# A decode attention kernel that streams its cache through a five-slot ring: slots handed out by the program, w_down in one load, two small loads swapped, one more V tile halved

## The chip, the core and the metric

The kernel runs on one core of one Trainium2 chip. The metric is the device time of one execution in microseconds; the time of a kernel is the median of its runs. The core has a matrix engine (TensorE, PE in the profile), a vector engine (VectorE, DVE), a scalar engine (ScalarE, ACT), GpSimd (POOL), a queue processor that issues transfers (SyncE, SP) and 16 DMA engines, which carry every load from the chip's main memory (HBM) into the on-chip memory (SBUF).

## What is computed

One token is decoded. Part A is attention with 32 heads of width 128 over a cache of 65,536 positions, part B is a small gated feed-forward layer, and a sigmoid gate mixes the two:

```python
q = (x @ wq).reshape(32 heads, 128)             # x: 1 x 512, wq: 512 x 4096
scores = einsum("hd,hkd->hk", q, k_cache) * 128 ** -0.5
p = softmax(scores)
a = einsum("hk,hkd->hd", p, v_cache).reshape(1, 4096) @ wo       # wo: 4096 x 512
b = (silu(x @ w_gate) * (x @ w_up)) @ w_down    # 512 x 1792 twice, 1792 x 512
g = sigmoid((x * gate_w).sum())
out = g * a + (1 - g) * b
```

All inputs are bf16. The K cache and the V cache are 537 MB each, and every byte of them is used once; everything else together is some 14 MB.

## The kernel before, in words

**Tiles.** A tile is 16,384 positions of one head: 128 partitions, 128 positions of 128 numbers on each, 32 KB per partition, 4 MB in all. There are four tiles per head (`G`) and 128 K tiles and 128 V tiles (`N`). Each is fetched by one instruction on SP's queue (`load`, L102 to L109, the transfer itself on L108); a tuple `cuts` can divide a tile into several transfers. K0 comes in two halves, V126 in two halves, V127 in five pieces (32, 32, 32, 16 and 16 of its 128 columns); all others come whole.

**The ring.** The big loads share a pool of five slots of 32 KB per partition (`ring`, L58, `big`, L69). In the order of the program they are: wq (the query weights), K0, K1, w_gate with w_up (`gu_t`), w_down (`wd_t`), then K2, K3, and from there K and V tiles in turn, and last the second half of wo (`load_wo_end`). A new tile can be loaded into a slot once everything that used the slot's last tenant is done. The pool chooses the slot: it takes the one whose last use stands earliest in the program. SP works its queue strictly in order, so a load that waits for its slot holds back all loads behind it. Each transfer also reports to one of eight semaphores, taken in turn; a transfer waits until the one eight places before it has landed.

**The steps.** A list `steps` (L344 to L352) fixes what happens together: step n loads K tile n and, from n = 4 on, a V tile v which lags four tiles behind. From n = 40 on (`SPREAD`) a V tile is left out of some steps, until the lag is eight (`LAG`); the last eight steps have V tiles alone. In a step, DVE multiplies the K tile by the query in place (L240) and adds halves together down to a width of 16 (L244, `products`); PE adds the remaining 16 columns with an identity matrix into the scores (L254, `scores`). After the four tiles of a head come a maximum, an exponential on ACT (L279) and the sum (L288). PE multiplies V tiles by the probabilities (L302, `values`, 32 matmuls per tile). On PE the order within a step is: the finished head's column (`head_column`, L323), `values(v)`, then `scores(n)`, then the projection of a finished head with wo (L335, `project`). wo's first 16 heads come in four loads of 512 KB (`load_wo`, L167), the first of them in step 3; the last 16 heads come in five pieces behind V127 (L161).

**The feed-forward layer.** `feed_forward_in` (step 1) does the two first products, `feed_forward_mid` (step 2) silu, the product and the multiplication with w_down, `feed_forward_out` (step 3) the gate and the first addition into the final accumulator. For the multiplication with w_down the hidden vector is first rearranged from 128 partitions x 14 to 64 x 28 (L200 to L206), because w_down lies on 64 partitions, 28 rows of 1 KB each. It is loaded in eight transfers of eight partitions (L142 to L146); two of them are issued before K2, six behind K2.

**The small loads.** xT (x, 1 KB) is issued by ACT's queue at the very start (L76); it feeds `X_bc` (four copies on DVE, L91), which the query matmuls (L117) need. gwT (gate_w, 1 KB) is issued on SP's queue behind w_up (L149); it is first used in step 2 (L197).

**The end.** After V127's last matmul: `head_copy` of head 31 in two halves on ACT and DVE, four projections, head 31's column, twelve projections with wo's last half, a cast (L413) and the store of the output (L414).

Of the kernel before, what the change touches and what calls it, by code (L numbers as in the profile page):

```python
# [8 lines left out]
ACT = mybir.ActivationFunctionType  # L9
ALU = mybir.AluOpType  # L10
AXIS = mybir.AxisListType
P = 128
# [3 lines left out]
NB = 128  # L16
SLOTS = 5
# [8 lines left out]
def kernel(  # L26
# [14 lines left out]
    nc = tc.nc  # L41
    bf16 = mybir.dt.bfloat16
    f32 = mybir.dt.float32

    _, H, Sk, Dh = A_k_cache.shape
    D = A_x.shape[2]
    F = B_w_gate.shape[1]
    KT = D // P
    FT = F // P
    G = Sk // (NB * P)  # L50
    NBH = Sk // P
    N = H * G
# [2 lines left out]
    scale = float(Dh) ** -0.5  # L55

    consts = ctx.enter_context(tc.tile_pool(name="consts", bufs=1))
    ring = ctx.enter_context(tc.tile_pool(name="ring", bufs=SLOTS))  # L58
    small = ctx.enter_context(tc.tile_pool(name="small", bufs=2))
    ppool = ctx.enter_context(tc.tile_pool(name="ppool", bufs=3))  # L60
    wo_pool = ctx.enter_context(tc.tile_pool(name="wo_pool", bufs=2))
# [3 lines left out]
    psum_m = ctx.enter_context(tc.tile_pool(name="psum_m", bufs=2, space=bass.MemoryType.PSUM))  # L65

    ctx.enter_context(tc.manual_schedule())

    def big(name):  # L69
        return ring.tile([P, NB * Dh], bf16, name=name, tag="big")  # L70


    xT = consts.tile([P, KT], bf16, name="xT")
    gwT = consts.tile([P, KT], bf16, name="gwT")
    with nc.allow_non_contiguous_dma(reason="small"):
        nc.scalar.dma_start(out=xT, in_=A_x[0, 0, :].rearrange("(p t) -> p t", t=KT))  # L76
    wq_t = big("wq_t")
    wq_sb = wq_t[:, : KT * H * Dh].rearrange("p (t f) -> p t f", t=KT)
    nc.sync.dma_start(out=wq_sb, in_=A_wq.rearrange("(p t) f -> p t f", t=KT))

    ident_f = consts.tile([P, P], f32, name="ident_f")
    make_identity(nc, ident_f[:])
    ident_b = consts.tile([P, P], bf16, name="ident_b")
# [15 lines left out]

    K_tiles, V_tiles, S_tiles, P_tiles, O_tiles = {}, {}, {}, {}, {}  # L100

    def load(dst, cache, n, name, cuts=(0, NB)):  # L102
        h, g = divmod(n, G)
        t = big(name)
        view = t.rearrange("p (j d) -> p j d", d=Dh)
        src = cache[0, h, g * NB * P : (g + 1) * NB * P, :].rearrange("(p j) d -> p j d", j=NB)
        for a, b in zip(cuts[:-1], cuts[1:]):
            nc.sync.dma_start(out=view[:, a:b, :], in_=src[:, a:b, :])  # L108
        dst[n] = view  # L109

    load(K_tiles, A_k_cache, 0, "K_t", (0, NB // 2, NB))
    load(K_tiles, A_k_cache, 1, "K_t")

    def queries(g):
        qg_ps = psum_m.tile([P, QG * Dh], f32, name="qg_ps", tag="misc")
# [13 lines left out]
        queries(g)  # L129


    gu_t = big("gu_t")
    wgu_sb = gu_t[:, : 2 * KT * F].rearrange("p (w t f) -> p w t f", w=2, t=KT)
    nc.sync.dma_start(out=wgu_sb[:, 0], in_=B_w_gate.rearrange("(p t) f -> p t f", t=KT))
    nc.sync.dma_start(out=wgu_sb[:, 1], in_=B_w_up.rearrange("(p t) f -> p t f", t=KT))
    wd_t = big("wd_t")
    HP = P // 2
    GT = F // HP
    wd_sb = wd_t[:HP, : GT * D].rearrange("p (t n) -> p t n", t=GT)
    wd_rows = B_w_down.rearrange("(p t) n -> p t n", t=GT)  # L140

    def load_wd(*which):  # L142
        for i in which:
            lo = (0, 1, 2, 3, 32, 33, 34, 35)[i]
            part = slice(lo, lo + 29, 4)
            nc.sync.dma_start(out=wd_sb[part], in_=wd_rows[part])  # L146

    with nc.allow_non_contiguous_dma(reason="small"):
        nc.sync.dma_start(out=gwT, in_=gate_w.rearrange("(p t) -> p t", t=KT))  # L149
    load_wd(0, 1)  # L150
    WG = 4
    wo_tiles = {}

    WH = H // 2
    wo_end = []

    def load_wo_end(cuts):
        t = big("wo_t")[:, : (H - WH) * D].rearrange("p (h n) -> p h n", n=D)
        rows = A_wo[WH * P :, :].rearrange("(h p) n -> p h n", p=P)
        for a, b in zip(cuts[:-1], cuts[1:]):  # L160
            nc.sync.dma_start(out=t[:, a:b, :], in_=rows[:, a:b, :])  # L161
        wo_end.append(t)

    def load_wo(g):
        wo_tiles[g] = wo_pool.tile([P, WG, D], bf16, name="wo_sb")
        rows = A_wo[g * WG * P : (g + 1) * WG * P, :]
        nc.sync.dma_start(out=wo_tiles[g], in_=rows.rearrange("(h p) n -> p h n", p=P))  # L167
# [21 lines left out]
    def feed_forward_mid(gu_sb, eg):  # L189
        nc.vector.tensor_scalar_add(eg, eg, 1.0)  # L190
        nc.vector.reciprocal(eg, eg)
        hprod = consts.tile([P, FT], f32, name="hprod")
        nc.vector.tensor_tensor(out=hprod, in0=gu_sb[:, :FT], in1=eg, op=ALU.mult)
        hT = consts.tile([P, FT], bf16, name="hT")
        nc.vector.tensor_tensor(out=hT, in0=hprod, in1=gu_sb[:, FT:], op=ALU.mult)
        xg = consts.tile([P, KT], f32, name="xg")
        nc.vector.tensor_tensor(out=xg, in0=xT, in1=gwT, op=ALU.mult)  # L197
        xs = consts.tile([P, 1], f32, name="xs")
        nc.vector.tensor_reduce(out=xs, in_=xg, axis=AXIS.X, op=ALU.add)
        h_ps = psum_m.tile([HP, GT], f32, name="h_ps", tag="misc")  # L200
        for r in range(2):
            nc.tensor.matmul(
                h_ps[:, r * FT : (r + 1) * FT], lhsT=ident_b[:, r::2], rhs=hT, start=True, stop=True
            )
        h2 = consts.tile([HP, GT], bf16, name="h2")
        nc.scalar.activation(out=h2, in_=h_ps, func=ACT.Copy)  # L206
        b_ps = psum_m.tile([1, D], f32, name="b_ps", tag="misc")
        for t in range(GT):
            nc.tensor.matmul(  # L209
                b_ps, lhsT=h2[:, t : t + 1], rhs=wd_sb[:, t, :], start=(t == 0), stop=(t == GT - 1)  # L210
            )
        g_ps = psum_m.tile([P, 1], f32, name="g_ps", tag="misc")
        nc.tensor.matmul(g_ps, lhsT=ones_f, rhs=xs, start=True, stop=True)
        eg2 = consts.tile([P, 1], f32, name="eg2")
        nc.scalar.activation(out=eg2, in_=g_ps, func=ACT.Exp, scale=-1.0)
        return b_ps, eg2
# [13 lines left out]
    def products(n, a=0, b=NB):  # L230

        h = n // G
        K = K_tiles[n][:, a:b, :]
        qb = q_bc[:, h * Dh : (h + 1) * Dh]
        q_rep = bass.AP(
            tensor=qb.tensor,
            offset=qb.offset,
            ap=[list(qb.ap[0]), [0, b - a], [1, Dh]],
        )
        yield nc.vector.tensor_tensor(out=K, in0=K, in1=q_rep, op=ALU.mult)  # L240
        half = Dh
        while half > WIDTH:
            half //= 2
            yield nc.vector.tensor_tensor(  # L244
                out=K[:, :, 0:half], in0=K[:, :, 0:half], in1=K[:, :, half : 2 * half],
                op=ALU.add,
            )
# [97 lines left out]
    v = 0  # L345
# [8 lines left out]
    ff = done = tot_ps = None  # L354
    for n, v in steps:
        if n is not None and n > 1:
            load(K_tiles, A_k_cache, n, "K_t")
        if n == 2:
            load_wd(2, 3, 4, 5, 6, 7)
        if n == 3:  # L360
            load_wo(0)
        if v is not None:
            if v % (WG * G) == 2 * G and v // (WG * G) + 1 < WH // WG:
                load_wo(v // (WG * G) + 1)
            load(V_tiles, A_v_cache, v, "V_t", (0, NB) if v < N - 2 else (0, 64, NB) if v < N - 1 else (0, 32, 64, 96, 112, NB))
            if v == N - 1:
                load_wo_end((0, 4, 8, 12, 14, 16))
        if n == 2:
            ff = feed_forward_mid(*ff)
        halves = (0, NB // 2)  # L370
        vector = iter(()) if n is None else products(n)
        if n == 0:
            vector = (i for a in halves for i in products(n, a, a + NB // 2))
        top_of = None
        if n is None:
            top_of = H - 1 if S_tiles else None
        elif n % G == 0 and n > 0:
            top_of = n // G - 1
            vector = (i for a in halves for i in products(n, a, a + NB // 2))
        if top_of is not None:  # L380
            next(vector, None)
            mT_ps = row_max(top_of)
            next(vector, None)
            exponentials(top_of, mT_ps)
        for _ in vector:
            pass
        if n == 1:
            ff = feed_forward_in()
        if n == 3:
            feed_forward_out(*ff)  # L390
        if tot_ps is not None:
            weight(*tot_ps)
            tot_ps = None
        if done is not None:
            head_column(done, head_copy(done))
        if v is not None:
            values(v)
        if top_of is not None:
            tot_ps = top_of, total(top_of)
        if n is not None:  # L400
            scores(n)
        if done is not None and done < WH:
            project(done)
        done = v // G if v is not None and v % G == G - 1 else None
# [40 lines left out]
```

## Time and profile before

| | us |
|---|---|
| median of three runs (2533.16 to 2534.53) | 2533.54 |
| the profiled execution, its own time | 2534.51 |
| its span (first to last instruction) | 2532.6 |
| DVE busy in the span | 2175.5 |
| PE busy in the span | 1742.4 |
| ACT busy in the span | 75.9 |

The 16 DMA engines moved 1088.63 MB in the span, 430 GB/s in the mean. SP's queue carried 42,674 packets, which fill 99.7% of the 16 engines' time; 53 packets of 16 KB are instructions which the engines' own programs fetch. The mean granted clock of TensorE was 0.749 of full speed.

The profile gives busy times by engine and line, a picture of the span in 40 slices, the waits (who waited for whom), the chain of work that ended last, and a timeline. Times are microseconds from the start of the span. The trace also holds two lists which the views add up: one row for every packet of every DMA engine (start, duration, bytes), and the completion marks of the transfers. Each DMA engine that takes part in a transfer posts its own mark when its share has landed, so a transfer that runs on 16 engines has 16 marks, and the transfer counts as landed with the last of them. Neither list names the engine.

### The profile page before, as it was taken

How to read it: one execution, taken by the hardware profiler on the slowest of the kernel's cores; microseconds unless marked ns; L12 is line 12 of the kernel's file. 1: busy time of each engine (PE TensorE's matmuls, PEld its weight loads, DVE VectorE, ACT ScalarE, POOL GpSimd, SP SyncE). 2: the span in 40 equal slices, each digit the busy share in tenths (PEclk: the TensorE clock that was granted, in tenths of full speed). 3: DMA queues.
4: the chain of work that ended last, by engine and by line, in shares of the span. 5: the costliest groups of instructions: out<-in, count | busy, mean ns of one | idle time of the engine just before them, and what ended most of it. 6: DMA issues, size and time to landing. Idle time of an engine off the chain costs nothing.

```text
span 2532.6 us, 15260 instructions
## 1 busy us (share of the span) xinstructions
PE 1742.4 (69%) x6738; PEld 712.1 (28%) x6738; DVE 2175.5 (86%) x784; ACT 75.9 (3%) x207; POOL 0.7 (0%) x6
## 2 busy tenths in 40 slices
PE   4677666776677666676776677667666776677679
PEld 2222222222222222222222223222222232222223
DVE  7998888888888999998888888888888888888860
ACT  1000000000000000000000000000000000000000
POOL 0000000000000000000000000000000000000000
PEclk7677777777777676677777777777777777777779
DMA  9999999999999999999999999999999999999998
GB/s 415 433 433 430 433 433 433 432 430 435 432 432 434 431 433 432 432 433 433 432 434 433 432 434 433 432 432 434 432 431 434 433 430 434 434 431 433 434 432 339
DMA packets 42884, 1088.63 MB, mean 430 GB/s; under 512 B 4737, under 2 KB 8834, under 8 KB 9090
## 3 DMA queue, kind: packets, MB, share of 16 engines
q1 hardware_dynamic: 42674, 1087.66, 99.7%
q8 instruction: 53, 0.87, 0.1%
q14 instruction: 13, 0.11, 0.0%
q10 hardware_dynamic: 144, 0.00, 0.0%
HBM read 1087.64 MB, written 0.00 MB: 429 GB/s over the span
## 4 chain that ended last, share of the span: by engine, by line
DMA 68%; PE 22%; DVE 10%; issue 1%; ACT 0%; DVEq 0%; SPq 0%
DMA V_t<-in_A_v_cache_dram 61%; PE O_ps L302 20%; DMA K_t<-in_A_k_cache_dram 5%; DVE K_t L240 5%; DVE K_t L244 5%; PE S_ps L254 1%; DMA wo_t<-in_A_wo_dram 1%; DMA wq_t<-in_A_wq_dram 0%; PE qg_ps L117 0%; DVE m L266 0%; PE oh_ps L323 0%; PE a_ps L335 0%; PE a_ps L227 0%; ACT P_sb L279 0%; DVE top L275 0%
## 5 line engine op out<-in xcount | busy, mean ns | idle before, releaser
L302 PE MATMUL O_ps<-V_t,P_sb 128*4 128x512 bf16 x4096 | 1157.3, 453 | 496.8 <-DMA V_t<-in_A_v_cache_dram 494.3
L240 DVE TENSOR_TENSOR K_t<-K_t,q_bc 128x16384 bf16<-128x16384 bf16 (+1 forms) x160 | 1117.2, 6983 | 254.4 <-DMA K_t<-in_A_k_cache_dram 232.9
L244 DVE TENSOR_TENSOR K_t<-K_t 128x4096 bf16<-128x4096 bf16 (+3 forms) x480 | 1030.9, 2148 | 14.3
L302 PEld LDWEIGHTS <-P_sb 128*4 128x4 bf16 x4096 | 393.9, 97 | 1241.0 <-issue 897.5
L254 PE MATMUL S_ps<-K_t,ident_b 128*128 128x128 bf16 x2048 | 466.0, 394 | 107.0 <-DVE K_t L244 106.9
L254 PEld LDWEIGHTS <-ident_b 128*128 128x128 bf16 x2048 | 227.6, 115 | 330.0 <-issue 140.2
L323 PE MATMUL oh_ps<-ident_f,O_sb 4*128 4x1 f32 x256 | 57.9, 343 | 74.1 <-ACT O_sb L315 74.1
L323 PEld LDWEIGHTS oh_ps<-ident_f,O_sb 4*128 4x128 f32 x256 | 55.2, 314 | 83.7 <-ACT O_sb L315 78.9
L270 PE MATMUL mT_ps<-diag,ones_f 128*128 128x128 f32 x64 | 23.6, 468 | 79.8 <-ACT diag L268 79.8
L268 ACT ACTIVATE diag<-ident_f,m 128x128 f32<-128x128 f32 x32 | 12.8, 401 | 2099.3 <-DVE m L266 2099.3
L317 DVE COPY O_sb<-O_ps 4x256 f32<-4x256 f32 x1 | 0.4, 414 | 52.1 <-ACT O_sb L315 52.1
L270 PEld LDWEIGHTS mT_ps<-diag,ones_f 128*128 128x128 f32 x64 | 14.7, 285 | 95.6 <-ACT diag L268 95.6
L266 DVE TENSOR_REDUCE m<-S_ps 128x1 f32<-128x512 f32 x32 | 21.9, 683 | 7.4 <-PE S_ps L254 7.4
L315 ACT ACTIVATE O_sb<-O_ps 4x512 f32<-4x512 f32 (+1 forms) x32 | 18.1, 566 | 131.0 <-PE O_ps L302 131.0
L279 ACT ACTIVATE P_sb<-S_ps,bias 128x512 bf16<-128x512 f32 x32 | 22.0, 687 | 1.0
L117 PE MATMUL qg_ps<-wq_t,X_bc 128*128 128x512 bf16 x32 | 8.6, 436 | 13.2 <-DMA wq_t<-in_A_wq_dram 13.2
L293 DVE RECIPROCAL recip<-tot_ps 128x1 f32<-128x1 f32 x32 | 5.1, 160 | 12.2 <-PE tot_ps L288 12.2
L209 PE MATMUL b_ps<-wd_t,h 64*1 64x512 bf16 x28 | 12.1, 629 | 4.3 <-DMA K_t<-in_A_k_cache_dram 4.3
L288 PEld LDWEIGHTS tot_ps<-rowsum,ones_f 128*128 128x128 f32 x64 | 9.5, 188 | 14.0 <-issue 14.0
L288 PE MATMUL tot_ps<-rowsum,ones_f 128*128 128x1 f32 x64 | 12.2, 260 | 0.0
L330 ACT ACTIVATE oT<-oh_ps,rg 128x1 bf16<-128x1 f32 x32 | 8.4, 263 | 76.6 <-PE oh_ps L323 76.6
L227 PE MATMUL a_ps<-b_sb,ones_f 1*1 1x512 f32 x2 | 1.9, 1032 | 12.1 <-ACT b_sb L226 12.1
(42 smaller groups left out, 73.8 us busy)
## 6 DMA issues: line engine op xcount, KB each, us to landing
K_t<-in_A_k_cache_dram SPq DMA_DIRECT2D x127, 4096.0 KB, 35.3
V_t<-in_A_v_cache_dram SPq DMA_DIRECT2D x126, 4096.0 KB, 29.1
wq_t<-in_A_wq_dram SPq DMA_DIRECT2D x1, 4096.0 KB
K_t<-in_A_k_cache_dram SPq DMA_DIRECT2D x2, 2048.0 KB, 16.8
V_t<-in_A_v_cache_dram SPq DMA_DIRECT2D x2, 2048.0 KB
V_t<-in_A_v_cache_dram SPq DMA_DIRECT2D x3, 1024.0 KB, 29.4
wo_sb<-in_A_wo_dram SPq DMA_DIRECT2D x4, 512.0 KB, 17.3
gu_t<-in_B_w_gate_dram SPq DMA_DIRECT2D x1, 1792.0 KB
```

What stands on the lines that cost most here:

```text
L209: nc.tensor.matmul(b_ps, lhsT=h2[:, t : t + 1], rhs=wd_sb[:, t, :], start=(t == 0), stop=(t == GT - 1))
L240: yield nc.vector.tensor_tensor(out=K, in0=K, in1=q_rep, op=ALU.mult)
L244: yield nc.vector.tensor_tensor(out=K[:, :, 0:half], in0=K[:, :, 0:half], in1=K[:, :, half : 2 * half], op=ALU.add,)
L254: nc.tensor.matmul(S_tiles[h][:, g * NB : (g + 1) * NB], lhsT=ident_b, rhs=K_tiles[n][:, :, c], start=(c == 0), stop=(c == WIDTH - 1),)
L266: nc.vector.tensor_reduce(out=m, in_=S_tiles[h], axis=AXIS.X, op=ALU.max)
L268: nc.scalar.activation(out=diag, in_=ident_f, func=ACT.Copy, scale=m)
L270: nc.tensor.matmul(mT_ps, lhsT=ones_f, rhs=diag, start=True, stop=True)
L279: nc.scalar.activation(out=P_tiles[h], in_=S_tiles[h], func=ACT.Exp, bias=bias, scale=scale, accum_out=rowsum[:, h : h + 1],)
L288: nc.tensor.matmul(tot_ps, lhsT=ones_f, rhs=rowsum[:, h : h + 1], start=True, stop=True)
L302: nc.tensor.matmul(O_tiles[h], lhsT=P_tiles[h][:, g * NB + j : g * NB + j + 4], rhs=V_tiles[n][:, j : j + 4, :], start=(g == 0 and j == 0) ...
L315: nc.scalar.activation(out=O_sb[:, :cut], in_=O_ps[:, :cut], func=ACT.Copy)
L323: nc.tensor.matmul(oh_ps, lhsT=O_sb[:, c * Dh : (c + 1) * Dh], rhs=ident_f[0:4, c : c + 1], start=(c == 0), stop=(c == 3),)
```

## The change

There are six edits.

1. The ring becomes one SBUF tile of five units, and the program itself gives out the units in rotation: allocation number i takes unit i mod 5. Nothing else decides about slots. Which instruction waits for which is still derived from the ranges that instructions read and write.
2. w_down is loaded by one transfer onto 128 partitions, 14 rows (14,336 bytes) each, behind K2 in step 2. The rearrangement of the hidden vector (two small matmuls, one copy on ACT) is gone, and the 28 matmuls with 64 partitions become 14 with 128.
3. xT moves from ACT's queue to SP's, behind wq.
4. gwT moves from SP's queue (behind w_up) to ACT's, at the very start.
5. The first load of wo moves from step 3 to step 6, there behind K6.
6. V125 comes in two halves, as V126 did already.

```diff
-    ring = ctx.enter_context(tc.tile_pool(name="ring", bufs=SLOTS))
...
-    def big(name):
-        return ring.tile([P, NB * Dh], bf16, name=name, tag="big")
+    UNIT = NB * Dh
+    ring = consts.tile([P, SLOTS * UNIT], bf16, name="ring")
+    taken = []
+
+    def big():
+        u = len(taken) % SLOTS
+        taken.append(u)
+        return ring[:, u * UNIT : (u + 1) * UNIT]
...
-        nc.scalar.dma_start(out=xT, in_=A_x[0, 0, :].rearrange("(p t) -> p t", t=KT))
+        nc.scalar.dma_start(out=gwT, in_=gate_w.rearrange("(p t) -> p t", t=KT))
     wq_sb = wq_t[:, : KT * H * Dh].rearrange("p (t f) -> p t f", t=KT)
     nc.sync.dma_start(out=wq_sb, in_=A_wq.rearrange("(p t) f -> p t f", t=KT))
+    with nc.allow_non_contiguous_dma(reason="small"):
+        nc.sync.dma_start(out=xT, in_=A_x[0, 0, :].rearrange("(p t) -> p t", t=KT))
...
-    wd_t = big("wd_t")
-    HP = P // 2
-    GT = F // HP
-    wd_sb = wd_t[:HP, : GT * D].rearrange("p (t n) -> p t n", t=GT)
-    wd_rows = B_w_down.rearrange("(p t) n -> p t n", t=GT)
-
-    def load_wd(*which):
-        for i in which:
-            lo = (0, 1, 2, 3, 32, 33, 34, 35)[i]
-            part = slice(lo, lo + 29, 4)
-            nc.sync.dma_start(out=wd_sb[part], in_=wd_rows[part])
-
-    with nc.allow_non_contiguous_dma(reason="small"):
-        nc.sync.dma_start(out=gwT, in_=gate_w.rearrange("(p t) -> p t", t=KT))
-    load_wd(0, 1)
+    wd_t = big()
+    wd_sb = wd_t[:, : FT * D].rearrange("p (t n) -> p t n", t=FT)
...
-        h_ps = psum_m.tile([HP, GT], f32, name="h_ps", tag="misc")
-        for r in range(2):
-            nc.tensor.matmul(
-                h_ps[:, r * FT : (r + 1) * FT], lhsT=ident_b[:, r::2], rhs=hT, start=True, stop=True
-            )
-        h2 = consts.tile([HP, GT], bf16, name="h2")
-        nc.scalar.activation(out=h2, in_=h_ps, func=ACT.Copy)
-        b_ps = psum_m.tile([1, D], f32, name="b_ps", tag="misc")
-        for t in range(GT):
-            nc.tensor.matmul(
-                b_ps, lhsT=h2[:, t : t + 1], rhs=wd_sb[:, t, :], start=(t == 0), stop=(t == GT - 1)
-            )
+        b_ps = psum_m.tile([1, D], f32, name="b_ps", tag="misc")
+        for ft in range(FT):
+            nc.tensor.matmul(
+                b_ps,
+                lhsT=hT[:, ft : ft + 1],
+                rhs=wd_sb[:, ft, :],
+                start=(ft == 0),
+                stop=(ft == FT - 1),
+            )
...
         if n == 2:
-            load_wd(2, 3, 4, 5, 6, 7)
-        if n == 3:
+            nc.sync.dma_start(out=wd_sb, in_=B_w_down.rearrange("(p t) n -> p t n", t=FT))
+        if n == 6:
             load_wo(0)
...
-            load(V_tiles, A_v_cache, v, "V_t", (0, NB) if v < N - 2 else (0, 64, NB) if v < N - 1 else (0, 32, 64, 96, 112, NB))
+            load(V_tiles, A_v_cache, v, (0, NB) if v < N - 3 else (0, 64, NB) if v < N - 1 else (0, 32, 64, 96, 112, NB))
```

## The prediction

> **What bounds the kernel.** I read the picture of the span first, then the waits, then the end of the timeline. The picture shows the DMA engines full in all slices but the last:
>
> ```profile
> DMA  9999999999999999999999999999999999999998
> GB/s 415 433 433 430 433 433 433 432 430 435 432 432 434 431 433 432 432 433 433 432 434 433 432 434 433 432 432 434 432 431 434 433 430 434 434 431 433 434 432 339
> q1 hardware_dynamic: 42674, 1087.66, 99.7%
> ```
>
> The waits agree: PE waits for V tiles, DVE for K tiles.
>
> ```profile
> PE O_ps L302 <- DMA V_t<-in_A_v_cache_dram: 494.3, 86, 7.4
> DVE K_t L240 <- DMA K_t<-in_A_k_cache_dram: 232.9, 101, 3.8
> ```
>
> The bytes stay the same. So only three things can move the time: how the bytes are shared among the 16 engines (a tile has landed when the last engine has its share), whether an engine ever waits for work, and the end behind the last tile. The timeline of the end (start, duration, what, count, and in brackets the idle time before and its cause):
>
> ```profile
> 2472.91 20.88 PE L302 MATMUL O_ps<-V_t,P_sb 128*4 128x512 bf16 x96
> 2495.45 7.07 PE L302 MATMUL O_ps<-V_t,P_sb 128*4 128x512 bf16 x32
> 2504.14 20.88 PE L302 MATMUL O_ps<-V_t,P_sb 128*4 128x512 bf16 x96 [1.62 <-DMA V_t<-in_A_v_cache_dram]
> 2527.00 2.75 PE L335 MATMUL a_ps<-wo_t,oT 128*1 128x512 bf16 x12
> 2529.79 0.68 DVE L413 CAST out_sb<-a_ps 1x512 bf16<-1x512 f32 x1 [3.85 <-PE a_ps L335]
> ```
>
> PE waits 1.62 us for V125 and then does V125 to V127 without a pause. The last windows show that not all engines are late (next to last column: DMA share; last: GB/s):
>
> ```profile
> 2506.00:2508.00 2.00, 2.00 (x11) 0.77 (x9) 0.00 (x0) 0.00 (x0) 0.00 (x0) 1.00 1.02 425
> 2510.00:2512.00 2.00, 2.00 (x11) 0.81 (x10) 0.00 (x0) 0.00 (x0) 0.00 (x0) 1.00 0.86 360
> 2520.00:2522.00 2.00, 2.00 (x11) 0.77 (x9) 0.00 (x0) 0.00 (x0) 0.00 (x0) 1.00 0.19 75
> ```
>
> The share is 0.19 while V127's last piece is still on its way. The completion marks say why. Sixteen engines finish a transfer at these distances from the first of them (us), from the trace's list of marks:
>
> ```
> K1            last 32.6    0 to 0.7, all sixteen
> K3            last 70.0    0 0 0 .1 .3 .3 .4 .4 | 8.3 8.4 8.4 8.4 8.5 8.7 8.8 9.9
> a tile        last 1133.4  0 .7 4.0 4.0 4.1 4.2 4.5 5.7 | 8.1 8.2 8.5 8.6 9.3 10.7 11.2 12.3
> V127, piece 5 last 2523.7  0 0 6.8 6.8 6.9 7.1 7.4 7.8 8.3 8.4 8.5 8.6 9.1 12.7 15.5 16.6
> ```
>
> Between K1 and K3 lies w_down. Its eight pieces have eight engine marks each and finish 1.06 us apart, so all eight pieces run on the same eight engines, which fall 8 x 1.06 = 8.5 us behind and never catch up. Later steps of about 1.2 to 1.5 us, one engine at a time, are the 53 instruction packets of 16 KB. I followed each engine from transfer to transfer: the three that end last (12.7, 15.5, 16.6) are all of w_down's eight; of the other eight, the latest ends at 8.5.
>
> **The change, part by part.**
>
> *w_down whole.* On 128 partitions it has 16 marks, like w_gate and w_up, which have its size (1792 KB) and ended at 36.9 and 41.1, K1 at 32.6: 4.25 us each on every engine. So w_down's eight engines gain 8.5 - 4.25 = 4.25 us, the others lose 4.25. Offsets at the end: latest of the first group 16.6 - 4.25 = 12.35, of the second 8.5 + 4.25 = 12.75. The last landing comes 16.6 - 12.75 = **3.85 us** earlier, and with it every V tile near the end. The last engine never waited for work: from K2 to V127, its previous transfer ended at least 12.5 us after SP issued the next. That the engines now run in step costs nothing: a 32 KB packet takes 1.213 us between 22 and 33 us (spread 0.7) and 1.213 us after 1000 us (spread 12 and more).
>
> The Trainium skill ("DMA: Bandwidth & Descriptors", Anatomy of one DMA) gives each transfer about 2.0 us of fixed cost; by it, seven transfers fewer and one more (V125) would make 12 us less. The pieces at 1.06 us apart, which is their bytes' time alone (28,672 bytes in 1.062 us), disagree, and the sum takes the row. The same page (Latency and other measured facts) calls engines 7 and 15 usually slower; were 15 the late one here, w_down would add 4.25 us to it (2537.8). The packets show no slow engine.
>
> *The rest of w_down.* Fourteen matmuls and the copy behind h_ps go; w_down lands at about 55.2 instead of 60.3, so its matmuls end near 62 instead of 72. PE waits for K tiles there; nothing on the path. Value: 0.
>
> *xT and gwT.* xT now lands behind wq, at about 13.4 (wq: 13.2) instead of 8.4. The four copies (0.63 us) then stand ahead of the queries, which end at about 22.9 instead of 21.86. Who waits: K2's load (slot of wq), needed when w_up ends at 41.1; and DVE's first product, which waits for K0's first half until 18.1, while the first four heads' queries are there by 16.8. Value: 0; without that cover 1 us. SP issues the same number of small loads, ACT as well.
>
> *wo's first load* (512 KB, 1.24 us of every engine) only changes places, and is needed in step 8. Value: 0.
>
> *Slots in rotation.* Before, a V tile took the slot of the V tile just multiplied, a K tile that of the K tile just scored:
>
> ```profile
> 2389.25 8.43 PE L302 MATMUL O_ps<-V_t,P_sb 128*4 128x512 bf16 x32
> 2397.72 0.33 SPq L108 DMA_DIRECT2D V_t<-in_A_v_cache_dram  x1
> 2397.86 3.64 PE L254 MATMUL S_ps<-K_t,ident_b 128*128 128x128 bf16 x16
> 2401.53 0.33 SPq L108 DMA_DIRECT2D K_t<-in_A_k_cache_dram  x1
> ```
>
> Counting five allocations back, V now takes the slot of a K tile and waits for its scores, usually 3.6 to 4 us longer, up to 8 where PE waits for DVE. I set each load to the release that rotation gives it, with the trace's times. The smallest reserve (last engine's previous landing minus issue) falls from 12.5 to 8.1 us at V2 and from 15.5 to 9.3 at V50. From issue to first packet some 1.2 us pass (wq: 0.74 to 1.95). At V2 the engines now come some 4 us earlier, but wo's load lies in front of it (1.24) and DVE is 0.8 earlier: some 4 us remain; at V50 5 to 6. Value: 0, and each microsecond beyond the reserve would be lost for good. The ranges in one big tile should not add waits: DVE's first product began at 18.15 on K0's first half while the second was still loading, so waits already go by ranges inside a tile.
>
> *V125 in halves.* PE starts the first half when V124 is done, so the 1.62 us go, if the rest follows. With all landings 3.85 earlier and 0.2175 us per matmul: PE ends V125 at 2505.6 and half of V126 at 2509.1, waits for its second half (2513.8 - 3.85 = 2509.95), and is held again by V127's third piece (2521.2 - 3.85 = 2517.35); V127 ends at 2520.8 instead of 2525.02. The last 4.73 us to the projections' end would give 2525.6. But wo's last piece, which landed at 2529.1, lands at 2525.25, and two matmuls (0.45) follow: 2525.7 instead of 2529.75. So most of the 1.62 is taken back by landings.
>
> **Sum:** -4.05 us, say -4.0: span 2532.6 to 2528.6, that execution 2534.51 to 2530.5. The median lies 0.97 below the profiled execution, so the median goes from 2533.54 to **2529.5**. A measurement of this kernel tells about 0.2% from no change, 5.1 us; the forecast is inside that.
>
> **Rivals.**
>
> *Another engine becomes last (0.08).* If one engine without w_down takes one instruction packet more (up to 1.5 us), the gain is 2.4: 2531.1. For it: six of the eight such engines take packets at 1.5 us each; against: instruction count and order hardly change.
>
> *The end is shorter still (0.09).* If the late landings do not hold PE (packets fall otherwise), all of 3.85 + 1.62 counts: 2528.0. Against: wo's last piece.
>
> *No gain (0.04).* If the late engines were not w_down's, the others' extra 4.25 would count: up to 2537.8. Against: the jump between K1 and K3.
>
> *Slower, by the slots (0.05).* One mechanism: a load is held longer than rotation asks, because the single tile's waits are coarser, or SP's order lets one late K hold V and K. Place: V2 and the stretch of steps 43 to 56, where K tiles come without V. It decides from some 4 us of delay. A load held one tile longer (9.7 us) loses 9.7 - 4 = 5.7 at V2 and 9.7 - 5.5, some 4, at V50; with the gain of 4.0 that is 2533.54 + 9.7 - 4.0 = 2539.2. Two tiles longer would pass the steady reserve too (15 - 1.2 - 19.4 = -5.6 us per V tile) and cost hundreds.
>
> **Numbers.** Forecast 0.74, own range 2528.7 to 2530.5. The range 2528.0 to 2532.0 takes in the forecast and the first two rivals. Faster by over 0.2% (below 2528.47): 0.09 and an edge of the forecast, 0.12; slower (above 2538.6): the last rival, 0.05; the rest 0.83.
>
> **What would show it.** Right: all sixteen marks within 2 us at K3; spread at V127 about 8.5 us; DMA share near 1 to about 2514, then steep; no wait before V125; projections end near 2525.7. Wrong: DMA share below 0.99 in a window before 2500, V loads with a growing wait, or the last landing not earlier.

## The result, and the profile after

After takes **2540.57 us** (median of ten runs, 2540.21 to 2540.65), before 2534.50 us beside it (ten runs, 2533.06 to 2536.08): a ratio of 1.0025, 95% interval 1.0015 to 1.0034. The forecast was 2529.5 us, the range 2528.0 to 2532.0. The change makes the kernel slower, and no rival had named the reason.

The picture of after's span, bytes per slice and the queue's share:

```profile
DMA  9999999999999999999999999999999999999998
GB/s 417 429 429 430 432 432 431 431 430 430 430 432 433 429 430 431 432 433 430 429 432 433 430 431 430 433 431 431 431 430 433 431 430 431 432 432 430 431 433 358
q1 hardware_dynamic: 42834, 1087.66, 99.8%
```

The engines are as full as before and no slice stands out. But slices 2 to 39 average 431.0 GB/s, in before 432.6: 0.37% less, everywhere. That is 9 us in 2500, and it is easy to read over. The waits (total us, times, longest) have grown alike for both consumers of the transfers, by 14.4 and 22.0 us:

```profile
PE O_ps L294 <- DMA ring<-in_A_v_cache_dram: 508.7, 91, 8.5
DVE ring L232 <- DMA ring<-in_A_k_cache_dram: 254.9, 104, 4.4
```

The end of after's timeline:

```profile
2479.26 20.88 PE L294 MATMUL O_ps<-ring,P_sb 128*4 128x512 bf16 x96
2501.80 17.43 PE L294 MATMUL O_ps<-ring,P_sb 128*4 128x512 bf16 x80
2519.66 7.07 PE L294 MATMUL O_ps<-ring,P_sb 128*4 128x512 bf16 x32 [0.43 <-DMA ring<-in_A_v_cache_dram]
2527.05 3.61 PE L294 MATMUL O_ps<-ring,P_sb 128*4 128x512 bf16 x16 [0.33 <-DMA ring<-in_A_v_cache_dram]
2532.91 2.75 PE L327 MATMUL a_ps<-ring,oT 128*1 128x512 bf16 x12
2535.69 0.68 DVE L405 CAST out_sb<-a_ps 1x512 bf16<-1x512 f32 x1 [4.11 <-PE a_ps L327]
```

The wait before V125 is gone, and the late waits are short, as predicted. Yet the projections end at 2535.7 instead of 2529.75. The completion marks (distances from the first of sixteen, us) say that w_down did what it was meant to do:

```
K3              last 66.1    0 to 0.6, one at 1.6          (before: two groups, up to 9.9)
V127, piece 5   last 2529.6  0 .2 .4 .7 1.0 2.3 3.1 7.7 9.7 9.7 10.0 10.1 11.2 11.3 11.3 11.3   (before: last 2523.7, up to 16.6)
```

The spread at the end is 5.3 us less, and still the last landing is 5.9 us *later*. So every engine is late: taken in order, all sixteen marks come 4.9 to 13.3 us later than in before. The trace's list of packets shows by how much each transfer is slower: between 300 and 2480 us a 32,768-byte packet takes 1213 ns in before (99.9% of them exactly that; packets that an instruction packet lengthens left out), and in after 1213 to 1226 ns, on average 1216.93. Eight packets a tile and 256 tiles make 8 x 256 x 3.92 ns = 8.0 us.

### The profile page after: what moved, and what is told of

The parts are those of the page before. It is cut to its first block, busy times and chain, and to the rows that moved or that the text cites. A ratio compares the mean times of both kernels' runs of the same rounds, so it can differ in the third digit from the quotient of the medians.

```text
span 2538.4 us, 15128 instructions
## 1 busy us (share of the span) xinstructions
PE 1734.4 (68%) x6722; PEld 709.6 (28%) x6722; DVE 2175.5 (86%) x784; ACT 75.7 (3%) x206; POOL 0.7 (0%) x6
## 4 chain that ended last, share of the span: by engine, by line
DMA 58%; PE 27%; DVE 14%; issue 1%; ACT 0%; SPq 0%; DVEq 0%
DMA ring<-in_A_v_cache_dram 53%; PE O_ps L294 19%; PE S_ps L246 8%; DVE ring L232 7%; DVE ring L236 6%; DMA ring<-in_A_k_cache_dram 5%; DMA ring<-in_A_wo_dram 1%; DVE m L258 0%; PE oh_ps L315 0%; PE a_ps L327 0%; PE a_ps L219 0%; ACT P_sb L271 0%; DVE top L267 0%; SPq L115 0%; ACT O_sb L307 0%
## 5 line engine op out<-in xcount | busy, mean ns | idle before, releaser
L294 PE MATMUL O_ps<-ring,P_sb 128*4 128x512 bf16 x4096 | 1156.5, 452 | 511.2 <-DMA ring<-in_A_v_cache_dram 508.7
L232 DVE TENSOR_TENSOR ring<-ring,q_bc 128x16384 bf16<-128x16384 bf16 (+1 forms) x160 | 1117.3, 6983 | 255.0 <-DMA ring<-in_A_k_cache_dram 254.9
L236 DVE TENSOR_TENSOR ring<-ring 128x4096 bf16<-128x4096 bf16 (+3 forms) x480 | 1031.0, 2148 | 14.3
L246 PE MATMUL S_ps<-ring,ident_b 128*128 128x128 bf16 x2048 | 465.7, 394 | 115.1 <-DVE ring L236 115.0
L315 PEld LDWEIGHTS oh_ps<-ident_f,O_sb 4*128 4x128 f32 x256 | 55.1, 314 | 83.4 <-ACT O_sb L307 78.6
L124 PE MATMUL qg_ps<-ring,X_bc 128*128 128x512 bf16 x32 | 8.4, 430 | 13.5 <-DVE X_bc L98 13.5
```

Source lines behind the costliest of these rows:

```text
L124: nc.tensor.matmul(qg_ps, lhsT=X_bc[:, t, :], rhs=wq_sb[:, t, g * QG * Dh : (g + 1) * QG * Dh], start=(t == 0), stop=(t == KT - 1),)
L236: yield nc.vector.tensor_tensor(out=K[:, :, 0:half], in0=K[:, :, 0:half], in1=K[:, :, half : 2 * half], op=ALU.add,)
L246: nc.tensor.matmul(S_tiles[h][:, g * NB : (g + 1) * NB], lhsT=ident_b, rhs=K_tiles[n][:, :, c], start=(c == 0), stop=(c == WIDTH - 1),)
L294: nc.tensor.matmul(O_tiles[h], lhsT=P_tiles[h][:, g * NB + j : g * NB + j + 4], rhs=V_tiles[n][:, j : j + 4, :], start=(g == 0 and j == 0) ...
L315: nc.tensor.matmul(oh_ps, lhsT=O_sb[:, c * Dh : (c + 1) * Dh], rhs=ident_f[0:4, c : c + 1], start=(c == 0), stop=(c == 3),)
```

## The experiments

Theory 1 was the one nearest to the failed sentence: the staggered groups (w_down's eight engines 8.5 us behind the other eight) had kept packets short, and engines in step slow each other down. Theory 2, the rival, was the ring (one tile, slots in rotation). Four kernels set the halves of the change apart.

**before_wd1** is before with w_down whole on 128 partitions (and its 14 matmuls), nothing else:

```
-    HP = P // 2
...
-    load_wd(0, 1)
+    wd_sb = wd_t[:, : FT * D].rearrange("p (t n) -> p t n", t=FT)
...
         if n == 2:
-            load_wd(2, 3, 4, 5, 6, 7)
+            nc.sync.dma_start(out=wd_sb, in_=B_w_down.rearrange("(p t) n -> p t n", t=FT))
```

> The kernel before with one part of the change alone: w_down whole on 128 partitions behind K2, without the rearrangement. Theory 1: packets at about 1.218 us, time 2539 to 2542, as in the changed kernel. Theory 2: packets at 1.213 us, and the gain of the prediction without V125's part: about 2530.

Measured: 2540.81 us, ratio 1.0024 (1.0015 to 1.0034), packets 1216.81 ns.

**after_pool** is after with the ring as a pool of five tiles again (`big()` returns `ring.tile(...)`):

> The changed kernel with one part undone: the ring is a pool again, which chooses the slots. Theory 1: as the changed kernel, 2540, packets at 1.218 us. Theory 2: packets at 1.213 us and the predicted time, 2529 to 2531.

Measured: 2540.91 us, 1.0024 (1.0014 to 1.0034), packets 1216.83 ns. The rotation costs nothing and w_down alone brings the whole loss: so far theory 1.

**after_wd8** is after with w_down in before's eight pieces; **before_ring** is before with the ring as one tile, given out in rotation:

> The changed kernel with one part undone: w_down comes again in eight transfers of eight partitions (two before K2, six behind it), with the rearranged hidden vector. Theory 1 (w_down whole lets the two groups of eight engines run in step, and engines in step slow one another's packets): the eight engines fall 8.5 us behind again, 32 KB packets take 1.213 us again (1.218 in the changed kernel), and the time is that of before less about 1.5 us for V125 in halves: 2532 to 2534. Theory 2 (the packets are slowed by the ring: its place in SBUF or the order of its slots): packets stay at 1.218 us, the last engine has 4 us more to carry than in the changed kernel: 2543 to 2545.

> The kernel before with one part of the change alone: one SBUF tile for the ring, its slots given out in rotation. Theory 1: packets at 1.213 us and a time within 0.5 us of before, about 2534. Theory 2: packets at about 1.218 us and some 10 us more, 2543 to 2546.

Measured: 2562.93 (1.0111, 1.0096 to 1.0127) and 2563.27 us (1.0113, 1.0099 to 1.0126), which neither theory had. SP's part of before_ring's timeline (start, duration, issue) and one line of SP's waits:

```profile
4.02 0.45 SPq L154 DMA_DIRECT2D gwT<-in_gate_w_dram  x1
41.34 1.47 SPq L151 DMA_DIRECT2D ring<-in_B_w_down_dram  x2
46.47 0.34 SPq L113 DMA_DIRECT2D ring<-in_A_k_cache_dram  x1
66.88 3.97 SPq L151 DMA_DIRECT2D ring<-in_B_w_down_dram  x6
```

```profile
SPq L151 <- DMA ring<-in_B_w_gate_dram: 32.5, 1, 32.5
```

In before, where w_down has a tile of its own, its first piece was issued at 8.41; here it waits 32.5 us for w_gate, which lies in another slot. A piece that takes every fourth partition of one shared tile is held to overlap its neighbours. The queue runs dry, and most of the 28.7 us go there: V1's last mark is 19.7 us later than in before (129.6 against 109.9), that of V127's last piece 28.6. The 8.9 us added in between are about what the slow packets cost in after (8.0 by the estimate above). The eight pieces and the one-tile ring do not go together; that is a second, separate effect. The stagger was lost in it as well (marks within 0.5 us at 88 us), so these two kernels' packets of 1216.9 ns still suited theory 1.

**stag8, stag4, stag2** put the stagger back into after, with w_down on 64 partitions and the rearranged hidden vector as in before. Eight, four or two pieces take eight adjacent partitions each (so that no false overlap is expected), and the other rows come in one load:

```
+    wd_cuts = (0, 8, 16, 24, 32, 40, 48, 56, 64)   # stag4: (0, 8, 16, 24, 32, 64); stag2: (0, 8, 16, 64)
...
+            part = slice(wd_cuts[i], wd_cuts[i + 1])
+            nc.sync.dma_start(out=wd_sb[part], in_=wd_rows[part])
```

> After, with w_down in eight pieces of 8 adjacent partitions (64 partitions in all, as in before, where the pieces had a stride of 4). Every other part of the change stays. Theory 1 (a stagger of 8.5 us between two groups of eight engines keeps the 32,768-byte packets at 1213 ns): packets 1213 ns in the whole span, completion marks in two groups of eight some 8.5 us apart from K3 on, last loads 6 to 9 us earlier than in after, 2533 to 2535 us. Theory 2 (the ring's one tile, the order of its slots or the moved small loads slow the packets): packets stay at 1217 to 1218 ns and the time at 2540 us or more. Adjacent partitions are expected to go without the wait that strided pieces had in the one tile (w_down's first piece is issued near 8 us, not at 41).

> As stag8, but only four pieces of 8 partitions, and the other 32 partitions in one load that all sixteen engines share: a stagger of 4 x 1.06 = 4.25 us. If any stagger of a few packets is enough: packets 1213 ns, and the engine that ends last is 2.1 us earlier than in before (its group has 6.4 instead of 8.5 us of w_down), so 2531 to 2533 us, below both kernels. If the stagger has to be near the whole 8.5 us: packets 1217 to 1218 ns, 2541 to 2543 us. A share of slow packets in between would give 2533 to 2540.

> As stag8, but two pieces of 8 partitions, and 48 partitions in one load: a stagger of 2.1 us. If a stagger of two packets is enough: packets 1213 ns, last engine 3.2 us earlier than in before, 2530 to 2532 us. If not: packets 1217 to 1218 ns, 2540 to 2542 us.

Measured: 2562.44, 2558.48 and 2553.28 us (1.0114, 1.0097, 1.0077). The first piece was issued at 7.26, as hoped, but PE waits for w_down until 78.6, and K5, whose slot is w_down's, with it (timeline of stag8):

```profile
78.61 12.10 PE L215 MATMUL b_ps<-ring,h 64*1 64x512 bf16 x28 [22.34 <-DMA ring<-in_B_w_down_dram]
```

A 28,672-byte packet to eight adjacent partitions takes 2960 ns on average, where before's eight with a step of four take 1062. The Trainium skill ("SBUF — State Buffer", Door 1: The DMA port swizzle) says that four neighbouring partitions share a port. By it eight engines crowd on two ports instead of eight, and the packets agree in direction, at 2.8 times the duration.

The times are spoilt by this, but stag8 decides all the same: between 88 and 126 us its marks stand in two groups of eight, 8.4 us apart, and its packets take 1213 to 1226 ns, on average 1216.7. **Theory 1 falls.**

**before_again** is before itself, profiled on that chip:

> The kernel before once more, profiled on the chip of these runs. If the 1213 ns belong to the kernel: the same packets again. If they belong to the chip or to the execution that was profiled: some of its packets above 1215 ns.

Measured: 2534.59 us, 1213.01 ns. The fast packets belong to the kernel.

Next came variants of before without late landings. **before_v125** has V125's halves alone (`v < N - 3`). **before_s0** has w_down in four pieces of 16 partitions, `(0, 61, 4), (1, 62, 4), (2, 63, 4), (3, 64, 4)`: no stagger. **before_s4** has four pieces of 8 and two of 16: half the stagger. **before_early** is before_wd1 with w_down issued ahead of K2.

> Before with one late edit alone: V125 loaded in two halves. Nothing is changed ahead of the last 30 us, so nothing that the transfers do at the start differs. Theory 1 (a stagger between two groups of engines) has fallen with stag8, where the groups stood 8.4 us apart and the packets were slow all the same. Theory 3 (how the loads between w_up and K3 are laid out decides): packets 1213 ns, 2532.5 to 2534.5 us. Theory 4 (an accident of the program as a whole, such as where its tensors lie, which any edit turns over): packets 1217 to 1218 ns, 2541 to 2544 us.

> Before with w_down in four pieces of 16 partitions (stride 4, on the same 64 partitions), which all sixteen engines share: no stagger, the slots and all else of before. Theory 3: if even sharing of w_down is what makes the packets slow, 1217 to 1218 ns and 2539 to 2541 us, as before_wd1. If it is rather w_down on 128 partitions, or in one transfer, 1213 ns, and the last engine comes 3.85 us earlier, as the prediction had it: 2530 to 2531.5 us. Theory 4: slow or not by accident.

> Before with w_down in four pieces of 8 partitions (4.25 us on eight engines) and two of 16 (2.1 us on all): a stagger of 4.25 us, without the late landing of stag4. If even sharing makes the packets slow by degrees: a share of slow packets in between, 2533 to 2538 us. If any uneven sharing keeps them at 1213 ns: last engine 2.1 us earlier, 2531.5 to 2533 us. If only the whole 8.5 us does: 1217 to 1218 ns, 2541 to 2542 us.

> Before with w_down whole on 128 partitions (as before_wd1), but issued right behind w_up, ahead of K2. In before_wd1 the packets were at 1213 ns up to 40 us and slow from K2 on. If w_down's place behind K2 is what matters: 1213 ns and 2530 to 2531.5 us. If even sharing matters, wherever it lies: slow from K2 on, 2540 to 2541.5 us.

Measured: before_v125 2534.37 us (0.9999, 0.9990 to 1.0008), before_s0 2536.34 (1.0008, 0.9999 to 1.0017), before_s4 2534.60 (1.0003, 0.9994 to 1.0011), all three with 1213.0 ns packets; before_early 2541.05 (1.0027, 1.0016 to 1.0038) with 1216.81. So before_s0 has no stagger at all, and fast packets. (It is not faster for another reason: its 28,672-byte packets take 1907 ns on average, up to 2276, instead of 1062, some 3.4 us more on each engine, and the first packets of K2 and K3 behind them 1.6 us more; together that is over the 3.85 to be gained.) What the four fast kernels share is not the order of the loads.

They share a small tile, h2, and with it the place where the ring begins in a partition of SBUF. In before the constant tiles lie ahead of the ring, from byte 16512 on; their sizes, each rounded up to 32 bytes, add up to 14,464, so the ring begins at 30976. h2 (56 bytes, kept as 64) is one of them, and it goes when w_down is whole; in after the ring moved ahead of them all, to 16512. Sorted by that place, each kernel's packets fall in line (300 to 2480 us, packets below 1260 ns; the last four columns are the shares of packets at these durations):

```
ring's first byte   over 256   kernels                                   mean ns   1213   1215   1218   1222
30976                  0       before, before_again, _v125, _s0, _s4    1213.00    99.9%   0      0      0
30912                192       before_wd1, before_early, after_pool     1216.8      5.8%  51%     2%    20%
16512                128       after, before_ring, after_wd8            1216.9     20-21% 11-12% 17-20% 3%
16512                128       stag8, stag4, stag2                      1216.7     23-26% 11-20%  6-16%  3-5%
```

The slots follow one another at 32,768 bytes, so all five share the remainder. That this remainder decides is theory 5 (3 and 4 are those of before_v125's expectation); its rival is that w_down's layout decides, since h2 goes with it. A pad alone tells them apart:

```
+    pad = consts.tile([P, 64], bf16, name="pad")    # after_al: 128 bytes ahead of the ring, 16512 -> 16640
+    pad = consts.tile([P, 192], bf16, name="pad")   # after_al512: 384 bytes, 16512 -> 16896
+    pad = consts.tile([P, 32], bf16, name="pad")    # 64 bytes: wd1_al (before_wd1), 30912 -> 30976
+                                                    #           before_mis64 (before), 30976 -> 31040
```

> After with an unused tile of 128 bytes a partition ahead of the ring, so that the ring begins at 16640, a multiple of 256, instead of 16512. Theory 5 (the ring's place decides the packets): 1213 ns in the whole span, and the change's own gain of about 4 us comes out: 2529 to 2531.5 us. Rival (w_down's layout decides): packets at 1217 to 1218 ns and 2540.5 us.

> before_wd1 (before with w_down whole and nothing else) with an unused tile of 64 bytes, so that the ring begins at 30976 again. Theory 5: 1213 ns, and w_down's even sharing is worth its 3.85 us: 2530 to 2531.5 us. Rival: 2540.8 us as before_wd1.

> Before with an unused tile of 64 bytes and nothing else: the ring begins at 31040, 64 over a multiple of 256. Theory 5: packets above 1213 ns by some 4 ns, times 8 packets times some 250 tiles, 8 to 10 us: 2542 to 2545 us. Rival: 1213 ns and 2534.5 us.

> After with an unused tile of 384 bytes: the ring begins at 16896, a multiple of 512. Theory 5: as after_al, 1213 ns and 2529 to 2531.5 us; nothing below 1213 ns is expected, since before's packets are the same 1213 ns from the first to the last. Rival: 2540.5 us.

Measured: after_al **2530.72 us** (0.9987, 0.9978 to 0.9996), wd1_al **2530.58** (0.9986, 0.9978 to 0.9995), after_al512 2530.70 (0.9986, 0.9977 to 0.9995), before_mis64 **2543.70** (1.0041, 1.0028 to 1.0054). Packets: 1213.0 ns in the first three, 1216.76 in before_mis64, with the pattern of the 192 row (6% at 1213, 52% at 1215, 20% at 1222). The rival falls. after_al differs from after by 128 unused bytes and is 9.85 us faster. A pad also moves the tiles behind it, but where the constant tiles lie does not matter: in before they begin at 16512, in after_al behind the ring at 180480 (remainders 128 and 0), and both kernels are fast. Bytes per slice, first of after_al, then of before_mis64:

```profile
GB/s 418 432 431 431 433 433 434 432 431 433 433 435 431 431 433 434 431 433 434 431 433 434 434 432 432 433 433 433 433 431 435 433 432 431 434 435 433 430 433 364
```

```profile
GB/s 416 431 429 429 432 432 430 432 428 432 431 430 433 429 431 430 433 429 432 431 430 433 432 429 434 430 431 432 431 431 432 431 432 430 430 430 432 432 430 324
```

The averages of slices 2 to 39 are 432.6 and 430.9, as in before and after. Last, the size: **before_mis128** has 128 bytes of pad in before (31104), **after_mis32** 32 bytes in after (16544, no multiple of 64).

> Before with an unused tile of 128 bytes: the ring begins at 31104, 128 over a multiple of 256, in before's pool. If the offset decides both the cost and the pattern: packet times as in after (some 20% at 1213 ns, 17% at 1218 ns, 12% at 1221 ns) and 2543 to 2545 us. If 128 over costs nothing by itself and after's slow packets needed the ring as one tile: 1213 ns and 2534.5 us.

> After with an unused tile of 32 bytes: the ring begins at 16544, 160 over a multiple of 256 and 32 over a multiple of 64. If only the multiple of 256 matters: packets near 1217 ns and 2540 to 2541 us, as after. If the cost grows as the offset gets finer (a row of 32,768 bytes then has one more piece at each finer size): above 2545 us.

Measured: 2543.78 us (1.0037, 1.0023 to 1.0052), 1216.90 ns and after's pattern (21% at 1213, 18% at 1218) for the first; 2540.37 (1.0023, 1.0013 to 1.0032) and 1216.86 ns for the second. The remainder sets the pattern; the mean is 3.8 to 3.9 ns over 1213 for 64, 128, 160 and 192 alike (3.7 in the stag kernels).

The Trainium skill ("DMA: Bandwidth & Descriptors", How a descriptor splits into AXI transactions) states that transactions start at multiples of 256 bytes, and that one which begins off such a place fetches the unused bytes too, in 32-byte beats. It speaks of reads; here the place written to was moved. Its multiple is the one found. As an estimate from that page, 2, 4, 5 and 6 beats on 1024 would be 2.4, 4.7, 5.9 and 7.1 ns at 64, 128, 160 and 192; the measured 3.8, 3.9, 3.9 and 3.8 do not grow so, and the measurement decides.

## Why the prediction was wrong

**The step that failed** is this sentence: "That the engines now run in step costs nothing: a 32 KB packet takes 1.213 us between 22 and 33 us (spread 0.7) and 1.213 us after 1000 us (spread 12 and more)." Its claim on engines in step holds (before_s0, wd1_al). What fails is what it was used for: it carried 1.213 us over into the changed kernel as if it were a property of the packet's size. It belongs to the size and to the place written to. The change moves that place from 30976 to 16512, and no step of the sum asked where the tiles lie. The missing term is +9.85 us (after against after_al); with after_al's gain of 3.77 us over before (2530.72 against 2534.49) that makes the 6.1 us by which after is slower. Summed over the packets of each length and divided by sixteen engines, after's 32,768-byte packets take 8.15 us more than after_al's, the 1024-byte ones 0.44, the instruction packets 0.43, the rest 0.34: 9.4 of the 9.7 us by which wo's last piece lands later (2535.0 against 2525.3).

**The other steps, with that term away.** The end of after_al's timeline:

```profile
2493.01 28.04 PE L295 MATMUL O_ps<-ring,P_sb 128*4 128x512 bf16 x128
2523.23 2.75 PE L328 MATMUL a_ps<-ring,oT 128*1 128x512 bf16 x12
2526.02 0.68 DVE L406 CAST out_sb<-a_ps 1x512 bf16<-1x512 f32 x1 [4.05 <-PE a_ps L328]
```

- *w_down whole, -3.85:* wd1_al is 3.91 us below before (2530.58 against 2534.49). wo's last piece lands at 2525.3 in after_al; the prediction said 2525.25.
- *V125 in halves, "most of the 1.62 is taken back by landings":* before_v125 gains 0.08 us. The wait itself changes from run to run: in before_again it is 0.16 us instead of 1.62, and the projections still end at 2529.9. PE does V124 to V127 of after_al without a wait (the x128 above), and the projections end at 2526.0, predicted 2525.7.
- *The rest of w_down, xT and gwT, wo's first load, the slots, all at 0:* after_al, which has them all, and wd1_al, which has w_down alone, are 0.14 us apart. after and after_pool are 0.34 apart.
- *The sum:* a span of 2528.6 was forecast; after_al's is 2528.8.
- *The 2.0 us per transfer and the slower engines 7 and 15, quoted from the Trainium skill:* the sum used neither, and after_al's span agrees with the sum without them. The page's 2.0 us stand under the path of transfers that GpSimd issues, and its guess at why engines 7 and 15 are slower is that path's descriptor rings; the loads here are issued by SP.
- *The spread at V127, "about 8.5":* 11.3 in after, 10.2 in after_al. So the per-engine account did not hold for all of the engines, and that the last landing agrees within 0.1 us (2519.9 in after_al, forecast 2519.8) is in part luck; the marks name no engine, so which ones differ is not shown.
- *"The ranges in one big tile should not add waits":* true for ranges along the row, false for partitions with a step (before_ring). In after no such piece is left, so it cost nothing there.
- *The rival "slower, by the slots"* gave 2539.2, near the result, but by another mechanism, so that is chance: after_pool, whose slots the pool chooses as in before, is as slow.
- *The range* had no room for a change in the packets' rate. 0.3% of a kernel that streams for 2.5 ms is more than all that was summed.

## What to carry to other kernels

When nearly all of the time is one kind of transfer, its duration is worth more than any wait: here 4 ns of 1213 made 8 of the 10 us. Look at where the big tiles begin in a partition before and after a change, since a small tile added or dropped ahead of them shifts them; begin them at a multiple of 256 bytes, by a pad if need be. When a result is off by a fraction of a per cent with no one wait to show for it, compare the durations of single packets, not the shares.

## What the runs showed of the hardware that was not expected

- Rows written at a place off a multiple of 256 bytes cost 3.7 to 3.9 ns more for 32,768 bytes, whatever the remainder (64, 128, 160 or 192); a multiple of 512 gives no more than one of 256.
- The cost is not always there, and why was not settled. In after, before_wd1 and before_mis64 K0 and K1 still ran at 1213 ns up to 33 us. In before_ring the packets fall back to 1213 ns (98% of them or more) for 24 to 26 us behind three of wo's loads (254 to 280, 568 to 592, 892 to 918 us) and then slow down again. after_wd8 and the three stag kernels have such stretches too; after, after_pool, before_wd1, before_early, before_mis64, before_mis128 and after_mis32 have none. The first five are the kernels in which w_down held up the queue at the start; what the one has to do with the other is open. So the offset makes packets open to some further delay rather than simply longer; which one, no run here tells. Work on DVE is not needed for it: between 2480 and 2500 us of after DVE does nothing, and packets take 1216.5 ns on average.
- Eight engines writing to eight adjacent partitions take 2960 ns on average for 28,672 bytes (stag8), to eight partitions with a step of four 1062 (before); sixteen engines on sixteen partitions with a step of four (before_s0) take 1907 on average, up to 2276.
